# Strided sparse attention and a rational MLP on one core: smaller score blocks, fewer and larger transfers, PSUM banks handed out by the planner, |h| on ScalarE

## The chip, the cores and the metric

The kernel runs on one NeuronCore of a Trainium2 chip. The metric is device time in microseconds (us): the median of several executions of the same program. One further execution was recorded by the hardware profiler; its rows are quoted below. The engines are named as in the profile: PE (TensorE matmul), PEld (its weight loads), DVE (VectorE), ACT (ScalarE), POOL (GpSimd) and SP (SyncE, which computes nothing here and only issues transfers). A q behind an engine's name means its queue: SPq L455 is a transfer that SP issues at line 455.

## The reference

Batch 8, 8 heads, 576 positions, head size 64. The first four heads see the last 32 positions, the other four see the earlier positions with the same remainder by 32. The attention result, 4608 tokens of 512 numbers, goes through an MLP with a rational activation of 2048 hidden columns.

```python
scores = (1/np.sqrt(D)) * np.matmul(q, k.transpose(0, 1, 3, 2))
rel = pos[:, None] - pos[None, :]
mask_local   = (rel >= 0) & (rel < 32)
mask_strided = (rel >= 0) & (pos[None, :] % 32 == pos[:, None] % 32)
# heads 0..3 local, heads 4..7 strided; masked scores are -1e9
attn = softmax(scores)                      # max subtracted, sum + 1e-9
x = (attn @ v).transpose(0, 2, 1, 3).reshape(B * S, H * D)

h = x @ w_in                                # 4608x512 by 512x2048
P = a[0] + a[1]*h + a[2]*h*h + a[3]*h*h*h
Q = 1 + abs(b[0])*abs(h) + abs(b[1])*h*h
out = (P / (Q + 1e-6)) @ w_out              # by 2048x512
```

## The kernel before, in words

**Transfers.** POOL casts q, k and v of each batch to bf16 in DRAM scratch (lq, lk: local heads in pairs; sq, sk: strided heads; v), seven transfers a batch, and loads both weights. SP then loads each batch: lqT and lkT by four transposing transfers (L428), the values of the local heads vL by six (L433), sqT and skT by eight transposes, one for each head of q and of k (L440), and the values of the strided heads vS by 32 (L455), each of 18 rows by 4 heads. POOL copies sqT into an order that matmul can use (sqP, L445).

**Attention.** A batch has six units: four local heads and two pairs of strided heads. A local head is six blocks of 96 queries by 128 keys; a strided pair is six blocks of 54 by 54 for even and for odd positions. In each unit PE writes a mask through the identity matrix (L481, L534) and adds the scores (L487, L540), DVE takes row maxima (L493, L547), PE adds the negated maxima (L499, L554), ACT takes the exponential (L505, L560), SP transposes the probabilities from SBUF to SBUF (pL to ptL, L509; pS to ptS, L564), PE multiplies by the values with a column of ones beside them (ps_acc, L516, L574), and DVE divides by that sum (L522, L524, L581, L583). Results of local heads are transposed from SBUF into the MLP's input xt (L615, 57 transfers in all); strided ones go to DRAM by POOL (xs, L592) and come back by transposes (L623).

**MLP.** The tokens form nine chunks of 512. For each, PE makes 16 blocks of 128 hidden columns (ps_h, L641) and ACT evicts each to h (L645). Eight blocks are a group: DVE makes |h| by a bit mask (L656), then the denominator (L658, L660); ACT takes Ln and Exp of it (L661, L663), which is its reciprocal; DVE makes the numerator (L664 to L669) and the product (L670). The second matmul (ps_out, L683) collects 16 steps for each of four blocks of 128 tokens; ACT copies it out (L688) and POOL stores it (L694).

**What sets the order.** Every step is an operation with an engine, an estimated duration and a key. A planner in the kernel simulates the engines and picks on each the ready operation with the smallest key; the resulting order is written out, and each engine runs it strictly in that order, waiting on semaphores. SP's order is such a list as well, so a transfer whose data are late holds up all transfers behind it. PSUM is split into fixed rings: two score tiles of two banks (ps_s), one bank for ps_acc, two for ps_h, one for ps_out.

Of the kernel before, what the change touches and what calls it, by code (L numbers as in the profile page):

```python
# [22 lines left out]
class Op:  # L23

    __slots__ = ("eng", "maker", "dur", "deps", "key", "dst", "dma", "gen", "ndep", "users",
                 "ready", "fin", "cnt", "idx", "know")

    def __init__(self, eng, maker, dur, key, dst, dma):
        self.eng = eng
        self.maker = maker  # L30
        self.dur = dur
        self.key = key
        self.dst = dst
        self.dma = dma
        self.gen = None
        self.deps = {}
        self.users = []


class Tile:  # L40


    def __init__(self, name, t=None):
        self.name = name
        self.t = t
        self.prev = []
        self.w = []
        self.r = []
        self.gen = 0
        self.ndma = {}  # L50
        self.sem = None

    def new(self):
        self.prev = self.w + self.r
        self.w = []
        self.r = []
        self.gen += 1
        return self


class Prog:
# [6 lines left out]
    def op(self, eng, maker, dur, key, r=(), w=(), m=(), dma=None):  # L68
        o = Op(eng, maker, dur, key, None, dma)
# [7 lines left out]
        for t in m:  # L77
            for d in t.w + t.r:
                o.deps[d] = 1
        for t in r:  # L80
            t.r.append(o)
        for t in w:
            t.w.append(o)
        for t in m:
            t.w = [o]
            t.r = []
        if dma is not None:
            assert len(w) == 1
            o.dst = w[0]
            o.gen = w[0].gen  # L90
            o.dst.ndma[o.gen] = o.dst.ndma.get(o.gen, 0) + 1
# [3 lines left out]

    def schedule(self):
        for o in self.ops:
# [4 lines left out]
        pend = {e: [] for e in self.ENG}  # L102
        avail = {e: [] for e in self.ENG}
        free = {e: 0.0 for e in self.ENG}
        order = {e: [] for e in self.ENG}
        dmafree = 0.0
        for o in self.ops:
            if o.ndep == 0:
                heapq.heappush(pend[o.eng], (0.0, o.key, o.idx, o))
        left = len(self.ops)  # L110
        while left:
            best = None
            for e in self.ENG:
                if avail[e]:
                    t = free[e]
                elif pend[e]:
                    t = max(free[e], pend[e][0][0])
                else:
                    continue
                if best is None or t < best[0]:  # L120
                    best = (t, e)
            t, e = best
            while pend[e] and pend[e][0][0] <= t:
                _, k, i, o = heapq.heappop(pend[e])
                heapq.heappush(avail[e], (k, i, o))
            _, _, o = heapq.heappop(avail[e])
            free[e] = t + o.dur
            if o.dma is not None:
                dmafree = max(dmafree, t + o.dur) + o.dma
                o.fin = dmafree + 2.2  # L130
# [3 lines left out]
            left -= 1  # L134
            for u in o.users:
                lat = 0.07 if u.eng == o.eng else 0.15
                u.ready = max(u.ready, o.fin + lat)
                u.ndep -= 1
                if u.ndep == 0:
                    heapq.heappush(pend[u.eng], (u.ready, u.key, u.idx, u))  # L140
        self.order = order
        self.span = max(free.values())

    def emit(self):
# [26 lines left out]
        while len(done) < total:  # L171
            moved = False
            for e in self.ENG:
                while ptr[e] < len(self.order[e]):
# [5 lines left out]
                    for d in sorted(o.deps, key=lambda d: -d.idx):  # L180
                        if d.eng == "pe" and e == "pe":
# [10 lines left out]
                    ws = [(semof[s], n) for s, n in need.items()]  # L192
                    queues[e].append((ws, o))
# [3 lines left out]
            assert moved, "order is cyclic"  # L197

        def run(e):
            def go(eng):  # L200
                for ws, o in queues[e]:
# [5 lines left out]
                    elif inst is not None:  # L207
                        inst.then_inc(sems[e], 1)
            return go
        fin = {}  # L210
        for o in self.ops:
            if o.dma is not None and not o.users:
                fin[o.dst.sem] = max(fin.get(o.dst.sem, 0), o.cnt)

        def pool(eng):
            run("pool")(eng)
            for s, n in fin.items():
                eng.wait_ge(s, n)
        with nc.Block() as block:
            block.sync(run("sp"))  # L220
            block.gpsimd(pool)
# [5 lines left out]
class Ring:  # L227
    def __init__(self, tiles):
        self.tiles = tiles
        self.i = 0  # L230
# [6 lines left out]

def bass_strided_sparse_attn__then__act_rational_pade_kernel(nc, q, k, v, moe_w_in, moe_w_out, moe_a, moe_b, out):
    w_in, w_out, pa, pb = moe_w_in, moe_w_out, moe_a, moe_b
    B, H, S, D = q.shape  # L240
    Fin = H * D
    Fmid = w_in.shape[1]
    Fout = w_out.shape[1]
# [513 lines left out]
```

## Time and profile before

| | |
|---|---|
| median of 3 executions | 778.47 us (777.2 to 779.21) |
| profiled execution, span | 779.0 us |
| busy | PE 395.9, PEld 178.2, DVE 362.0, ACT 267.7, POOL 141.1 us |
| instructions | 6110, of them 2304 matmuls |
| DMA | 58.44 MB in 186076 packets, 179552 of them under 512 B |

The span is the time from the first to the last instruction of the profiled execution, and its own time; it lies 0.5 us above the median. A busy time is the sum over an engine's instructions; issuing transfers does not count as busy, so SP has no busy time, and what its queue costs shows in the chain of work that ended last (where SPq stands for SP's issuing) and in the waits for its transfers. In the slices, each digit is a fortieth of the span, in tenths busy. PE's clock is granted by a throttle; 1.00 is full speed.

### The profile page before, as it was taken

The numbers are of one execution on the slowest core, as the hardware profiler recorded it, in microseconds if no ns is written. First come the engines' busy times: TensorE is split into PE (matmuls) and PEld (weight loads), VectorE is DVE, ScalarE is ACT, GpSimd is POOL, SyncE is SP. The second block draws the span as 40 slices with busy tenths as digits, with TensorE's granted clock in tenths as the row PEclk, the third lists the DMA queues.
The fourth block names the chain that finished last, engine by engine and source line by source line (L and its number), as shares of the span: only waits on it lengthen the run. The fifth ranks groups of instructions, "written<-read, shape, count | busy, mean of one in ns | idle before, by whom it ended". The sixth has DMA issues, their size and how long they took to land.

```text
span 779.0 us, 6110 instructions
## 1 busy us (share of the span) xinstructions
PE 395.9 (51%) x2304; PEld 178.2 (23%) x2304; DVE 362.0 (46%) x353; ACT 267.7 (34%) x265; POOL 141.1 (18%) x184
## 2 busy tenths in 40 slices
PE   0212240401565010890169095789089959699864
PEld 0001120200222000340024042344034424233321
DVE  3000130100309104360298086489088959969960
ACT  0100000100126040262057044458138657577740
POOL 9007034005160100120003002022010400301100
PEclk9999999999997555795579588799579979999988
DMA  9999969218899042232301342352141321301011
GB/s 148 197 146 116 153 91 111 46 28 127 109 138 123 12 79 53 66 74 39 70 9 53 57 91 48 71 101 60 29 88 30 76 67 39 83 13 55 27 41 40
DMA packets 186076, 58.44 MB, mean 75 GB/s; under 512 B 179552, under 2 KB 182144, under 8 KB 185536
## 3 DMA queue, kind: packets, MB, share of 16 engines
q0 software_dynamic: 46144, 30.17, 23.3%
q1 hardware_dynamic: 139904, 27.90, 22.4%
q8 instruction: 18, 0.29, 0.2%
q14 instruction: 10, 0.08, 0.0%
HBM read 42.54 MB, written 25.95 MB: 88 GB/s over the span
## 4 chain that ended last, share of the span: by engine, by line
SPq 49%; PE 18%; DVE 17%; DMA 6%; ACT 4%; issue 4%; POOL 0%; DVEq 0%; ACTq 0%; POOLq 0%
SPq L455 24%; SPq L440 9%; PE ps_out L683 8%; PE ps_h L641 7%; SPq L615 7%; SPq L433 4%; SPq L428 4%; DVE z L666 3%; DVE z L668 3%; DMA ptL<-pL 3%; DVE h L670 2%; DVE u L660 2%; SPq L509 2%; DVE z L667 1%; ACT u L661 1%
## 5 line engine op out<-in xcount | busy, mean ns | idle before, releaser
L683 PE MATMUL ps_out<-Wout,h 128*128 128x512 bf16 x576 | 148.3, 411 | 25.6 <-ACT os L688 13.1
L641 PE MATMUL ps_h<-xt,Win 128*128 128x512 bf16 x576 | 144.2, 403 | 22.2 <-ACT h L645 9.4
L645 ACT ACTIVATE h<-ps_h 128x512 bf16<-128x512 f32 x144 | 85.0, 597 | 107.4 <-PE ps_h L641 107.3
L516 PE MATMUL ps_acc<-vL,ptL 128*96 128x65 bf16 x192 | 17.5, 237 | 165.3 <-DMA ptL<-pL 163.0
L505 ACT ACTIVATE pL<-ps_s 96x768 bf16<-96x768 f32 x32 | 25.7, 803 | 218.5 <-DMA ptL<-pL 121.4
L522 DVE RECIPROCAL rc<-ps_acc 96x6 f32<-96x6 f32 x32 | 6.1, 189 | 189.0 <-PE ps_acc L516 188.9
L694 POOL DMA_DIRECT2D out_dram<-os x36 | 26.5, 736 | 344.6 <-ACT os L688 340.2
L683 PEld LDWEIGHTS ps_out<-Wout,h 128*128 128x128 bf16 x576 | 57.0, 104 | 103.2 <-issue 17.1
L641 PEld LDWEIGHTS ps_h<-xt,Win 128*128 128x128 bf16 x576 | 52.0, 103 | 98.4 <-ACT h L645 30.4
L661 ACT ACTIVATE u<-u,consts 128x4096 bf16<-128x4096 bf16 x18 | 66.6, 3702 | 2.3 <-DVE u L660 2.2
L663 ACT ACTIVATE u<-u 128x4096 bf16<-128x4096 bf16 x18 | 65.1, 3618 | 0.1
L592 POOL DMA_DIRECT2D xs<-xS x48 | 35.4, 742 | 155.8 <-DVE xS L583 155.7
L493 DVE TENSOR_REDUCE ng<-ps_s 96x6 bf16<-96x768 f32 x32 | 30.3, 946 | 60.7 <-PE ps_s L487 60.6
L516 PEld LDWEIGHTS ps_acc<-vL,ptL 128*96 128x96 bf16 x192 | 15.6, 155 | 174.1 <-DMA ptL<-pL 166.9
L688 ACT ACTIVATE os<-ps_out 128x512 f32<-128x512 f32 x36 | 21.5, 596 | 98.6 <-PE ps_out L683 98.5
L481 PE MATMUL ps_s<-ML,IDN 128*96 128x512 bf16 x64 | 21.2, 423 | 57.4 <-DMA lkT<-lk 31.8
L445 POOL COPY sqP<-sqT 128x324 bf16<-128x324 bf16 x32 | 18.5, 620 | 128.0 <-DMA sqT<-sq 128.0
L390 POOL DMA_DIRECT2D lk<-in_k_dram x16 | 41.4, 3070 | 0.0
L524 DVE TENSOR_TENSOR xL<-ps_acc,rc 96x384 bf16<-96x384 f32 x32 | 17.6, 549 | 51.2 <-DMA xt<-xs 48.7
L660 DVE TENSOR_TENSOR u<-u,z 128x4096 bf16<-128x4096 bf16 x18 | 41.1, 2286 | 0.3
L666 DVE TENSOR_TENSOR z<-z,h 128x4096 bf16<-128x4096 bf16 x18 | 41.0, 2279 | 0.2
L670 DVE TENSOR_TENSOR h<-z,u 128x4096 bf16<-128x4096 bf16 x18 | 41.1, 2282 | 0.1
(41 smaller groups left out, 474.5 us busy)
## 6 DMA issues: line engine op xcount, KB each, us to landing
out_dram<-os POOLq DMA_DIRECT2D x36, 256.0 KB, 2.5
v<-in_v_dram POOLq DMA_DIRECT2D x8, 576.0 KB, 10.3
vS<-v SPq DMA_DIRECT2D x256, 9.0 KB
vL<-v SPq DMA_DIRECT2D x48, 64.0 KB, 2.2
lq<-in_q_dram POOLq DMA_DIRECT2D x16, 144.0 KB, 11.5
lk<-in_k_dram POOLq DMA_DIRECT2D x16, 144.0 KB, 11.3
sq<-in_q_dram POOLq DMA_DIRECT2D x8, 288.0 KB, 10.6
sk<-in_k_dram POOLq DMA_DIRECT2D x8, 288.0 KB, 11.8
```

The costliest lines, as they stand in the source:

```text
L390: P.op("pool", lambda e, s_t=s_t, d_t=d_t: e.dma_start(d_t[b, pair, :, :].rearrange("s (hh d) -> s hh d", hh=2), s_t[b, 2 * pair:2 * pair ...
L440: P.op("sp", lambda e, t=t, d_t=d_t, h=h: e.dma_start_transpose(t.t[:, h, 0:S // 2], d_t[b, h, :, :].rearrange("(c two) d -> c (two d)", t ...
L455: P.op("sp", lambda e, i=i, par=par, blk=blk, base=base: e.dma_start(vS.t[base:base + 52:3, blk // 2, par, :, blk % 2, 0:64], bass.AP(tens ...
L615: P.op("sp", lambda e, t=t, r0=r0, n=n, col=col, i=i: e.dma_start_transpose(t.t[:, 0:2, col:col + n], xl.t[r0:r0 + n, i, :]), 0.15, key + ...
L641: r = e.matmul(ph.t[:, :], Win[:, kk, f * 128:(f + 1) * 128], xt.t[:, kk, :], start=(kk == 0), stop=(kk == NK1 - 1))
L645: P.op("act", lambda e, f=f, ph=ph, h=h: e.activation(h.t[:, f % G, :], ph.t[:, :], AF.Copy), 0.53, key, r=[ph], w=[h])
L660: dv(lambda e, zz=zz, uu=uu: e.tensor_tensor(uu, uu, zz, op=Alu.mult), tt, r=[z], m=[u])
L661: P.op("act", lambda e, uu=uu: e.activation(uu, uu, AF.Ln, bias=eps1, scale=1.0), 0.833 * W / 1000 + 0.28, key, r=[T_co], m=[u])
L663: P.op("act", lambda e, uu=uu: e.activation(uu, uu, AF.Exp, scale=-1.0), 0.833 * W / 1000 + 0.19, key, m=[u])
L666: dv(lambda e, zz=zz, hh=hh: e.tensor_tensor(zz, zz, hh, op=Alu.mult), tt, r=[h], m=[z])
L670: dv(lambda e, zz=zz, hh=hh, uu=uu: e.tensor_tensor(hh, zz, uu, op=Alu.mult), tt, r=[z, u], m=[h])
L683: r = e.matmul(po.t[:, :], groups[g].t[:, j, m * 128:(m + 1) * 128], Wout[:, kk, :], start=(kk == 0), stop=(kk == NF - 1))
```

## The change

It alters the local and strided blocks, the transfers, PSUM, and the MLP's |h|:

- **Local heads** become 18 blocks of 32 queries by 64 keys, all four heads in one unit: 72 small matmuls (L522), placed in 32-column tiles of the array, with the mask for all of them by three matmuls through the identity (L509, L510), one maximum (L546), two exponentials (L559, L563) and one transpose of the probabilities (L566).
- **Strided heads** become blocks of 36 queries by 36 keys: positions with the same remainder by 16, one parity at a time (64 matmuls a batch, L591), in two units of two heads. PE reads every eighth column of sqT in place; the copies sqP are gone.
- **Weighted sums** are 72 matmuls for the local (L635) and 64 for the strided heads (L687), each half held back by a wait of PE for itself (`hard`).
- **Transfers**: a batch is loaded by four transposes (L469, L475), six vL (L481, L486) and eight vS (L495). All results go to DRAM (L665, L669, L696) and one or two transposes bring them back as xt (L711). SP also issues these stores and the output stores (L801); POOL keeps casts and weights. Casts of batch b+2 wait for the first load of batch b+1.
- **PSUM**: instead of fixed rings, the planner hands out one to three of eight banks to each result at the moment at which it orders the result's first operation, and makes that operation wait for the last users of those banks.
- **MLP**: ACT makes |h| for 16 of the 18 groups (L746); |h|, Ln (L759) and Exp (L764) run in halves of 2048 columns; the output matmuls (L789) are ordered in pieces of four instead of eight. Rings: xt 2 instead of 3, h 5 instead of 6.
- The planner's durations and keys are others: batch b's attention has the key 33b-20, chunk c's MLP 33c+10.

```diff
+class Banks:                        # n banks, place chosen when ordered
+    def __init__(self, n):
+        self.n = n
...
     def schedule(self):
...
+            if o.bank is not None:
+                b = o.bank
+                at, f = self._place(b.n, t)
+                b.at = at
+                for i in range(at, at + b.n):
+                    for d in self.blast[i]:
+                        o.deps.setdefault(d, 1)
+                    self.bfree[i] = 1e9
...
-        for h in range(HL):
-            for t, d_t in ((tq, sq), (tk, sk)):
-                P.op("sp", lambda e, t=t, d_t=d_t, h=h: e.dma_start_transpose(
-                    t.t[:, h, 0:S // 2], d_t[b, h, :, :].rearrange("(c two) d -> c (two d)", two=2)),
+        for nm, R, d_t, T in (("sq", R_sq, sq, T_sq), ("sk", R_sk, sk, T_sk)):
+            P.op("sp", lambda e, t=t, d_t=d_t: e.dma_start_transpose(
+                t.t[:, :, :], d_t[b, :, :, :].rearrange("h (c two) d -> (h c) (two d)", two=2)),
...
-        for i in range(16):
-            for par in range(2):
-                P.op("sp", lambda e, i=i, par=par, blk=blk, base=base: e.dma_start(
-                    vS.t[base:base + 52:3, blk // 2, par, :, blk % 2, 0:64],
+        for r in range(2):
+            for h in range(HL):
+                P.op("sp", lambda e, r=r, h=h: e.dma_start(
+                    vS.t[64 * r:64 * r + CS, h, :, 0:64],
...
+            return e.matmul(bank(SL, c + 64 - n, n, po, po + 32),
+                            lqt.t[64 * hh:64 * hh + 64, pair, LB * m:LB * m + LB],
+                            lkt.t[64 * hh:64 * hh + 64, pair, k0:k0 + n],
+                            start=False, stop=True, skip_group_check=True, tile_position=(64 * hh, po))
...
+                            r = e.matmul(bank(SS, 512 * j + CS * r2, CS, p, p + CS),
+                                         sqt.t[p:p + 64, h, r2:S // 2:8], skt.t[p:p + 64, h, r2:S // 2:8],
...
+        o1 = P.op("pe", lambda e: lav(e, 0), 36 * 0.028, key, r=[ptL, vl], w=[AL])
+        P.op("pe", lambda e: lav(e, 1), 36 * 0.028, key, r=[ptL, vl], m=[AL], hard=[o1])
...
             P.op("sp", lambda e, t=t, r0=r0, n=n, col=col: e.dma_start_transpose(
-                t.t[:, 2:4, col:col + n], xs[b, r0:r0 + n, :]), 0.15, key + 10, ...
+                t.t[:, :, col:col + n], xs[b * S + r0:b * S + r0 + n, :]), 1.25, key, ...
...
+    ABS_ACT = set(range(2, 18))
...
+            if c * NG + g in ABS_ACT:
+                for i in range(2):
+                    P.op("act", lambda e, z=z, h=h, i=i: e.activation(
+                        z.t[:, half * i:half * i + half, :], h.t[:, half * i:half * i + half, :], AF.Abs),
...
-            P.op("pool", lambda e, o=o, u0=u0: e.dma_start(out[u0:u0 + 128, :], o.t[:, :]), ...
+            P.op("sp", lambda e, o=o, u0=u0: e.dma_start(out[u0:u0 + 128, :], o.t[:, :]), ...
...
         if b + 1 < B:
-            st = loads(b + 1)
-        xl = attention(b, cur)
-        gather(b, xl)
+            st = loads(b + 1, b * PER + 8)
+        if b + 2 < B:
+            casts(b + 2, b * PER + 6, after=[P.ops[n0]])
+        attention(b, cur, b * PER - 20)
+        gather(b, b * PER - 2)
```

How the order moves, at three places. A row gives the line, the operation, what it writes and reads, the shape and the count. First SP, around the transposes that bring batch 0's results back as xt; before:

```order
L440 DMA_TRANSPOSE skT<-sk 128x288
L433 DMA vL<-v 128x4x64 x6
L509 DMA_TRANSPOSE ptL<-pL 128x6x96
L615 DMA_TRANSPOSE xt<-xL 128x2x96 x5
L615 DMA_TRANSPOSE xt<-xL 128x2x32 x3
L564 DMA_TRANSPOSE ptS<-pS 128x6x128
L428 DMA_TRANSPOSE lqT<-lq 128x576
L428 DMA_TRANSPOSE lkT<-lk 128x576
```

and after, where the loads of batch 2 stand ahead of them:

```order
L696 DMA xs<-xS 288x1x256 x2
L469 DMA_TRANSPOSE lqT<-lq 128x2x576
L469 DMA_TRANSPOSE lkT<-lk 128x2x576
L475 DMA_TRANSPOSE sqT<-sq 128x4x288
L475 DMA_TRANSPOSE skT<-sk 128x4x288
L481 DMA vL<-v 32x2x64
L486 DMA vL<-v 64x17x64 x2
L481 DMA vL<-v 32x2x64
L486 DMA vL<-v 64x17x64 x2
L711 DMA_TRANSPOSE xt<-xs 128x4x512
L711 DMA_TRANSPOSE xt<-xs 128x4x64
L495 DMA vS<-v 36x16x64 x8
```

Ten loads of batch 2 now precede the two transposes to xt, and eight follow them. Second, PE around the first weighted sums of batch 0; before, they come behind the scores of batch 0's strided pairs and among those of its later local heads:

```order
L534 MATMUL ps_s<-MS,IDN 128x384 x2
L540 MATMUL ps_s<-skT,sqP 54x54 x24
L554 MATMUL ps_s<-ng,IDN 118x384 x2
L516 MATMUL ps_acc<-vL,ptL 96x65 x6
L481 MATMUL ps_s<-ML,IDN 96x512
L481 MATMUL ps_s<-ML,IDN 96x256
L487 MATMUL ps_s<-lkT,lqT 96x128 x6
```

and after (L608 and L578 ahead belong to batch 0's strided heads and to batch 1's mask, L522, L591 and L553 to batch 1):

```order
L608 MATMUL ps<-ng,IDN 100x288 x4
L578 MATMUL ps<-MS,IDN 128x288 x4
L522 MATMUL ps<-lkT,lqT 32x64 x4
L522 MATMUL ps<-lkT,lqT 32x32 x2
L522 MATMUL ps<-lkT,lqT 32x64 x6
L522 MATMUL ps<-lkT,lqT 32x32 x2
L522 MATMUL ps<-lkT,lqT 32x64 x58
L591 MATMUL ps<-skT,sqT 36x36 x64
L553 MATMUL ps<-ng,IDN 128x512 x2
L553 MATMUL ps<-ng,IDN 128x128
L608 MATMUL ps<-ng,IDN 100x288 x4
L635 MATMUL ps<-vL,ptL 32x65 x36
```

Batch 1's whole scores now stand ahead of batch 0's first weighted sum (L635). Third, PE in the middle of the program, where MLP and attention alternate; before:

```order
L683 MATMUL ps_out<-Wout,h 128x512 x16
L499 MATMUL ps_s<-ng,IDN 96x512
L499 MATMUL ps_s<-ng,IDN 96x256
L516 MATMUL ps_acc<-vL,ptL 96x65 x6
L683 MATMUL ps_out<-Wout,h 128x512 x16
L481 MATMUL ps_s<-ML,IDN 96x512
L481 MATMUL ps_s<-ML,IDN 96x256
L487 MATMUL ps_s<-lkT,lqT 96x128 x6
L516 MATMUL ps_acc<-vL,ptL 96x65 x6
L683 MATMUL ps_out<-Wout,h 128x512 x16
```

and after:

```order
L789 MATMUL ps<-Wout,h 128x512 x4
L608 MATMUL ps<-ng,IDN 100x288 x2
L731 MATMUL ps<-xt,Win 128x512 x20
L608 MATMUL ps<-ng,IDN 100x288 x2
L731 MATMUL ps<-xt,Win 128x512 x16
L789 MATMUL ps<-Wout,h 128x512 x4
L635 MATMUL ps<-vL,ptL 32x65 x36
L731 MATMUL ps<-xt,Win 128x512 x4
L635 MATMUL ps<-vL,ptL 32x65 x36
L789 MATMUL ps<-Wout,h 128x512 x4
```

The first and second matmuls of the MLP (L731, L789) now alternate in pieces of four, and a batch's local heads pass as two runs of 36 instead of four of six.

More of the change, by code (lines that the diff above doesn't have):

```diff
@@ L79, in op @@
                 o.deps[d] = 1
+        for d in tuple(after) + tuple(hard):
+            o.deps[d] = 1
+        o.hard = hard
         for t in r:
@@ L101, in schedule @@
                 d.users.append(o)
[L102 to L105, printed above, removed]
+            for b in o.banks:
+                b.left += 1
+        self.bfree = [0.0] * NBANK
+        self.blast = [[] for _ in range(NBANK)]
+        ready = {e: [] for e in E}
+        free = {e: 0.0 for e in E}
+        order = {e: [] for e in E}
         dmafree = 0.0
@@ L139, in schedule @@
                 if u.ndep == 0:
[L140 removed]
+                    ready[u.eng].append(u)
         self.order = order
[L142 removed]
+        self.span = max(o.fin for o in self.ops)
     def emit(self):
@@ L197, in emit @@
             assert moved, "order is cyclic"
+        fin = {}
+        for o in self.ops:
+            if o.dma is not None and not o.users:
+                fin[o.dst.sem] = max(fin.get(o.dst.sem, 0), o.cnt)
         def run(e):
@@ L316, in bass_strided_sparse_attn__then__act_rational_pade_kernel @@
     R_o = ring("os", 3, [128, Fout], f32)
-    def ps(name, shape):
-        return nc.alloc_psum_tensor(name, shape, f32)
-    R_ps = Ring([Tile(f"ps{i}", ps(f"ps_s{i}", [128, 2, 512])) for i in range(2)])
-    R_pa = Ring([Tile("pa0", ps("ps_acc", [128, 512]))])
-    R_ph = Ring([Tile(f"ph{i}", ps(f"ps_h{i}", [128, 512])) for i in range(2)])
-    R_po = Ring([Tile("po0", ps("ps_out", [128, 512]))])
-    qi = np.arange(128)[:, None]
-    ki = np.arange(128)[None, :]
-    ml = np.full((128, NTL, 128), NEG, np.float32)
@@ new lines, in casts, with local, bulk @@
+    def casts(b, key, after=()):
+        for t in (T_lq[b], T_lk[b], T_sq[b], T_sk[b], T_v[b]):
+            t.new()
+        def local(pair, s_t, d_t, t):
+            P.op("pool", lambda e: e.dma_start(
+                d_t[b, pair, :, :].rearrange("s (hh d) -> s hh d", hh=2),
+                s_t[b, 2 * pair:2 * pair + 2, :, :].rearrange("hh s d -> s hh d")),
+                2.8, key, w=[t], dma=(1.2, 3.0), after=after)
+        def bulk(s_t, d_t, h0, nh, hd, t):
+            n = nh * S * D
@@ L697, in bass_strided_sparse_attn__then__act_rational_pade_kernel @@
-    casts(0)
-    weights()
-    for b in range(1, B):
-        casts(b)
+            if not hasattr(o, "st"):
+                o.st = Tile(f"st{o.name}")
+            o.st.new()
+            P.op("sp", lambda e, o=o, u0=u0: e.dma_start(out[u0:u0 + 128, :], o.t[:, :]), 0.5, ky + m * 7.6 + 7,
+                 r=[o], w=[o.st], dma=(0.8, 2.5))
+    PER = 33.0
+    casts(0, -100)
+    weights_in(0, -90)
+    weights_in(1, -89)
+    casts(1, -80)
+    gates = {}
     nxt = 0
-    st = loads(0)
-    pend = []
+    st = loads(0, -50)
```

815 lines of the change are left out of this document (431 added, 384 removed).

## The prediction

> **What bounds the kernel now.** I read the page's span, slices and chain first, then the SP queue line by line, the PE waits, two stretches, and last the durations that price the new parts.
>
> ```profile
> span 779.0 us, 6110 instructions
> ...
> PE   0212240401565010890169095789089959699864
> ...
> SPq 49%; PE 18%; DVE 17%; DMA 6%; ACT 4%; issue 4%; POOL 0%; DVEq 0%; ACTq 0%; POOLq 0%
> SPq L455 24%; SPq L440 9%; PE ps_out L683 8%; PE ps_h L641 7%; SPq L615 7%; SPq L433 4%; SPq L428 4%; DVE z L666 3%; DVE z L668 3%; DMA ptL<-pL 3%; DVE h L670 2%; DVE u L660 2%; SPq L509 2%; DVE z L667 1%; ACT u L661 1%
> ```
>
> The chain that ends last runs 49% through SP's queue: not through bytes, but through the time in which SP issues transfers. The costliest line is L455, the value loads of the strided heads. PE is nearly idle for the first 11 of 40 slices. What one issue costs (nanoseconds, min/median/max; the last row is the landing time of the ptL transposes in us):
>
> ```profile
> L428 SPq DMA_TRANSPOSE lqT<-lq x16: 1146/1263/11241, 11.2 to 527.9; - x16
> L433 SPq DMA_DIRECT2D vL<-v x48: 389/507/4978, 28.9 to 573.7; - x48
> L440 SPq DMA_TRANSPOSE sqT<-sq x32: 1149/1245/5744, 47.4 to 335.0; - x32
> L455 SPq DMA_DIRECT2D vS<-v x256: 737/741/1022, 41.6 to 560.5; - x128
> L509 SPq DMA_TRANSPOSE ptL<-pL x32: 1197/1237/4629, 80.1 to 669.7; - x32
> L615 SPq DMA_TRANSPOSE xt<-xL x57: 1159/1241/3992, 185.1 to 685.5; - x57
> L623 SPq DMA_TRANSPOSE xt<-xs x16: 1212/1264/1302, 218.9 to 673.1; - x16
> DMA to landing us min/median/max: 2.5/2.6/10.9
> ```
>
> A transpose costs SP about 1.25 us whether it moves 288x128 (L440), 576x128 (L428) or 512x256 (L623). With some 0.04 us between issues, a batch costs SP 4x1.30 (lq, lk) + 6x0.55 (vL) + 8x1.29 (sq, sk) + 32x0.78 (vS) + 6x1.29 (pt) + 57/8x1.28 + 2x1.30 = 63 us; eight make 504 us of the 779. Behind that queue PE waits for probabilities that are long computed:
>
> ```profile
> PE ps_acc L516 <- DMA ptL<-pL: 163.0, 10, 23.8
> ```
>
> Two stretches (length, busy us of PE, PEld, DVE, ACT, POOL, then the granted clock, DMA share, GB/s) show the middle, paced by SP, and the end, where SP is done and DVE works 104.27 of 112 us, 93%:
>
> ```profile
> 224.00:640.00 416.00, 237.00 (x1431) 108.65 (x1430) 222.77 (x216) 172.57 (x169) 53.98 (x73) 0.76 0.35 64
> 640.00:752.00 112.00, 92.61 (x442) 38.20 (x441) 104.27 (x75) 79.10 (x75) 14.99 (x18) 0.95 0.15 42
> ```
>
> **The change, part by part.** The prices of SP's start and of PE's work:
>
> ```profile
> 13.96 11.24 SPq L428 DMA_TRANSPOSE lqT<-lq  x1
> 25.24 3.58 SPq L428 DMA_TRANSPOSE lkT<-lk  x1
> 28.94 12.61 SPq L433 DMA_DIRECT2D vL<-v  x6
> ...
> 60.20 19.87 SPq L455 DMA_DIRECT2D vS<-v  x25
> 80.11 5.92 SPq L509 DMA_TRANSPOSE ptL<-pL  x2
> ```
>
> ```profile
> 224.43 15.48 PE L641 MATMUL ps_h<-xt,Win 128*128 128x512 bf16 x64
> ...
> 587.98 0.71 PE L540 MATMUL ps_s<-skT,sqP 64*54 64x54 bf16 x24
> ...
> 649.41 0.42 PE L516 MATMUL ps_acc<-vL,ptL 128*96 128x65 bf16 x6
> 649.67 3.62 PE L641 MATMUL ps_h<-xt,Win 128*128 128x512 bf16 x16
> 653.22 0.36 PE L574 MATMUL ps_acc<-vS,ptS 118*64 118x130 bf16 x6
> ```
>
> *SP per batch.* 4 load transposes, 3 of probabilities and about 2 gathers (15 in all): 9x1.30 = 11.7 us. 6 vL x0.55 = 3.3. 8 vS, each eight times the old one's bytes: between 0.55 (a 64 KB vL) and 2.1 (a vL of the congested start, 12.61/6); I take the median of the shape they are nearest to, 0.78: 6.3. The output stores and the xs stores, taken over from POOL, 4.5 + 5 at 0.55: 5.2. Sum 26.5 us against 63 (24 to 39 by the bounds). SP stops being the bound once an engine needs more than that per batch. POOL keeps only the casts; the sqP copies are gone. New is that SP stands still at an output store until ACT has made the copy, and behind it stand the next loads and the next gather, for which PE waits: 16 us of SP's slack a batch (PE's 43, below, less 26.5) cover that; without them each such wait goes straight to PE. The bytes grow (vS fills both partition halves, and all of x goes through DRAM instead of half of it); the DMA share of 0.15 to 0.35 in the two stretches hides that.
>
> *The first MLP matmul,* now at 224.43 us, waits for three batches of loads in SP's order. Loads of batch 0: lq and lk are the same bytes as the four old transposes, issued by 28.8 us. sq and sk: 12 (3 if uncongested, 17.6 at the rate of the first pair). vL: 8 (3 to 19). vS: 6. Three pt transposes: 4. That makes 59. Loads of batch 1: 4x1.30 + 3.3 + 6.3 = 15 clean, and about 7 more if casts are in flight, since the two ptL at 80.11 took 2.96 each instead of 1.24: 81. PE does batch 1's scores before batch 0's weighted sums, so SP next waits for landing, scores, maxima and exponentials: about 9, by which ptL(1) goes out at 90. xs stores and ptS: 6, so 96. Ten loads of batch 2: 8.5 clean, I take 12: 108. Gather: 2.6 and a landing of 2.5 to 10.9, say 6. First MLP matmul at **117 us** (100 if nothing is congested, 140 if everything runs at the worst rates).
>
> *PE from there.* A 512-column matmul at full clock takes (653.22-649.67)/16 = 0.222 us; 1152 of them 256 us. Per batch, attention has 272 small matmuls: 136 scores like L540, 0.71/24 = 0.030 each; 136 weighted sums between 0.030 and L574's 0.060, I take 0.035, because they stream 65 columns, not 130, and load 32 to 64 weight columns, not 96 as L516 does (0.26/6 = 0.043). Sum 8.8 (8.2 to 12.2). Masks and maxima: 4608 columns by identity at 0.222 per 512: 2.0. Four waits of PE for itself: 0 to 1, say 0.5. 11.3 a batch, with an eighth of the 256 43 us of PE. Batches 3 to 7 and the weighted sums of 1 and 2 remain: 5x11.3 + 2x5 = 66. Together **322 us**.
>
> DVE and ACT (busy us in all, mean ns of one, then idle time before):
>
> ```profile
> L660 DVE TENSOR_TENSOR u<-u,z 128x4096 bf16<-128x4096 bf16 x18 | 41.1, 2286 | 0.3
> ...
> L493 DVE TENSOR_REDUCE ng<-ps_s 96x6 bf16<-96x768 f32 x32 | 30.3, 946 | 60.7 <-PE ps_s L487 60.6
> ...
> L656 DVE TENSOR_SCALAR z<-h 128x4096 uint16<-128x4096 uint16 x18 | 21.9, 1216 | 18.5 <-ACT h L645 18.3
> L583 DVE TENSOR_TENSOR xS<-ps_acc,rc 118x384 bf16<-118x384 f32 x32 | 17.6, 551 | 0.3
> ```
>
> ```profile
> L645 ACT ACTIVATE h<-ps_h 128x512 bf16<-128x512 f32 x144 | 85.0, 597 | 107.4 <-PE ps_h L641 107.3
> L661 ACT ACTIVATE u<-u,consts 128x4096 bf16<-128x4096 bf16 x18 | 66.6, 3702 | 2.3 <-DVE u L660 2.2
> L663 ACT ACTIVATE u<-u 128x4096 bf16<-128x4096 bf16 x18 | 65.1, 3618 | 0.1
> L505 ACT ACTIVATE pL<-ps_s 96x768 bf16<-96x768 f32 x32 | 25.7, 803 | 218.5 <-DMA ptL<-pL 121.4 <-PE ps_s L499 96.9
> ```
>
> *DVE.* The nine MLP groups from L660 to L656 take 15.6 us for 8 x 512 hidden columns; without |h| 14.4. 18 groups: 259, plus two |h| left: 2.4. Attention by elements: 2304 of maxima at 946/768 and 3200 of normalising at 551/384, some 7.5 with the reciprocals; six batches: 45. **307 us**.
>
> *ACT.* 144 evictions and 36 output copies at 0.6: 108. Ln and Exp 18x7.32, in halves with some 0.15 more each: 137. |h| by ACT is not in the trace; the nearest row is Exp, 3618, so 16x3.8 = 61 (0 to 3 less). Exponentials 2.4x6 = 14. **320 us** at most, since neighbours overlap.
>
> The Trainium skill (ScalarE: Activation LUTs, Rules for kernel authors) says that simple elementwise work belongs on VectorE, which is up to about three times as fast in bf16. The rows agree: 1216 ns against about 3618. By that rule |h| stays on DVE, which then needs 327 us and would set the end some 5 us later than PE does; so here the move pays a little although each |h| gets three times as dear.
>
> *The sum.* After the start the three engines need 322, 307 and 320 us: PE is the longest, barely. At the 93% that the longest engine reached from 640 to 752: 322/0.93 = 346 (322 at 100%, 379 at 85%). Handing out PSUM banks when ordered costs no instruction; I give it nothing, since up to eight results can now be open where four rings of one or two tiles were, and if its planned times are off, PE waits for evictions, which the 93% is to cover. The end: after the last MLP-1 matmul comes a group's chain on ACT and DVE, under which PE still has earlier output matmuls; about 8 us stay open, and 4 for eviction, store and landing. 117 + 346 + 12 = **475 us**. The profiled span, 779.0, stands 0.07% above the median of 778.47, so nothing is scaled.
>
> **The rivals.** *Small matmuls at L574's 0.060 each:* 4.1 us more for a batch's scores and 3.4 for its sums; five batches and two of sums make 44: (322+44)/0.93 = 394, so 523 us. For it: 32-column tiles at changing array positions are in no row. Against: L540, whose tiles change rows too, at 0.030. The Trainium skill (TensorE: Matmul & The Clock Gate, the section on 56 against 53.3 ns) gives about 62 ns per matmul where its sequencer decodes in firmware and 25 as the floor otherwise; with 62 the time would be an estimated 526 us. L540's 30 ns speaks against that.
>
> *A late start:* casts of batches 2 and 3 are now tied to loads that stand before the gather, so they collide with them; if transposes go at the 11.24 us of the row at 13.96, the first MLP matmul comes at 165: 523 us. Against: later medians are 1.24 to 1.26.
>
> *The engines take turns:* with all three near full, each wait is another's; PE pauses, and the granted clock falls to the 0.76 of 224 to 640: 322/0.76 = 424, 553 us. For it: that stretch. Against: its pauses came from SP.
>
> *Better cover:* an early start, 100, and PE never waiting: 434 us.
>
> *Slower than before:* if a merged transpose held SP 11.24 us in every batch, as one did at 13.96, nine would cost 101 us, with the rest 116 a batch, 930 in all. It decides from about 7.3 us a transpose, (779-117-12)/8 = 81 us a batch. Against it: three sizes at one price.
>
> **How the numbers follow.** The forecast has 58% (445 to 505), small matmuls 8%, a late start 12%, turns 11%, better cover 8%, slower 2%, no change 1%. From 445 to 535 lie the forecast, most of the first two rivals, and about a third of the turns, the milder ones: 80%. About 0.3% is what a measurement of this kernel can tell from no change. Faster 0.97, same 0.01, slower 0.02.
>
> **What will show it.** Right: no SP line among the chain's first; the first L731 matmul at 100 to 140; PE, DVE and ACT each over 80% busy after it; L522, L591, L635 and L687 starting 0.027 to 0.045 apart; L469 and L475 issued in about 1.25. Wrong: L469 or L475 at several us, L687 at 0.06, the clock under 0.85 after the start, or PE waiting for a bank's release or for ptL.

## The result

The changed kernel takes 589.5 us (median of 6 runs, 581.5 to 597.7), the kernel before, beside it, 778.6 (777.2 to 779.2): a ratio of 0.750, 95% interval 0.746 to 0.754. The ratios, here and below, go by the runs that were not disturbed (here 581.5 to 588.4 us), and where a text below says how many us a run is faster or slower, that is a difference of ratios times 778.6 us. The forecast was 475 us with a range from 445 to 535. It missed by 114 us.

The page of the changed kernel (its span, busy time of the engines, PE and DMA in 40 slices, the two large queues, q1 with SP's transfers and q0 with POOL's, the chain that ended last):

```profile
span 586.6 us, 7831 instructions
...
PE 349.3 (60%) x3393; PEld 167.0 (28%) x3440; DVE 314.7 (54%) x227; ACT 306.6 (52%) x317; POOL 61.5 (10%) x64
...
PE   1012105103552379087796597994898899996846
...
DMA  9999999979999999979959995795214414000101
...
q1 hardware_dynamic: 171744, 43.84, 57.2%
q0 software_dynamic: 41408, 18.35, 27.8%
...
SPq 37%; PE 16%; DVE 16%; ACT 16%; DMA 12%; issue 4%; POOL 0%; ACTq 0%; POOLq 0%
SPq L495 10%; SPq L486 8%; PE ps L731 8%; PE ps L789 6%; DMA xt<-xs 5%; ACT z L746 5%; SPq L481 5%; DMA xs<-xS 4%; SPq L469 4%; SPq L475 4%; ACT h L735 4%; ACT u L759 3%; DVE u L755 3%; ACT u L764 2%; DVE z L770 2%
```

SP still leads the chain, and its first two lines are value loads: L495 (vS) and L486 (vL). The row of DMA slices stands near 9 for the first two thirds of the span and then drops; PE's digits stay at 8 or 9 only after that.

Stretches of the changed kernel (length, busy us of PE, PEld, DVE, ACT, POOL, granted clock, DMA share, GB/s): first everything from the first MLP matmul on, then two stretches with loads and one without.

```profile
152.60:586.60 434.00, 322.74 (x2773) 149.82 (x2816) 299.99 (x203) 298.24 (x304) 30.00 (x28) 0.87 0.72 97
200.00:240.00 40.00, 24.89 (x102) 10.30 (x104) 16.98 (x10) 20.84 (x24) 6.94 (x7) 0.80 1.26 131
280.00:320.00 40.00, 32.95 (x318) 16.85 (x322) 29.91 (x21) 30.03 (x31) 6.02 (x7) 0.91 1.08 139
480.00:520.00 40.00, 38.90 (x179) 17.42 (x181) 34.94 (x22) 37.30 (x38) 0.00 (x0) 1.00 0.19 55
```

The work that the engines have from the first MLP matmul on came out as priced: PE 322.7 us (forecast 322), DVE 300.0 (307), ACT 298.2 (320). What they do not have is each other's company: 434 us for it, not 358. With loads the DMA share is above 1, because the times of the two queues' packets add up in it (0.89 of q1 and 0.37 of q0 from 200 to 240 us). So 1 is no ceiling: the kernel below with all of vS contiguous reaches 1.50 in that stretch. PE is busy 25 to 33 of 40 us there, and 38.9 without loads.

What SP's issues cost there (ns, min/median/max):

```profile
L469 SPq DMA_TRANSPOSE lqT<-lq x8: 1269/1638/5493, 8.9 to 365.2; - x8
L475 SPq DMA_TRANSPOSE sqT<-sq x8: 1244/1572/9984, 20.0 to 369.0; - x8
L486 SPq DMA_DIRECT2D vL<-v x32: 573/684/10984, 33.4 to 385.4; - x32
L495 SPq DMA_DIRECT2D vS<-v x64: 757/1200/4128, 63.4 to 395.4; - x64
```

And a batch in SP's timeline (start, length, what): the value loads of batch 3 with a gather between, and the first load of batch 4.

```profile
179.99 0.53 SPq L481 DMA_DIRECT2D vL<-v  x1
180.57 7.38 SPq L486 DMA_DIRECT2D vL<-v  x2
187.99 1.17 SPq L481 DMA_DIRECT2D vL<-v  x1
189.20 1.86 SPq L486 DMA_DIRECT2D vL<-v  x2
191.10 9.57 SPq L495 DMA_DIRECT2D vS<-v  x6
200.72 6.30 SPq L711 DMA_TRANSPOSE xt<-xs  x2
207.07 1.58 SPq L495 DMA_DIRECT2D vS<-v  x2
208.70 1.54 SPq L469 DMA_TRANSPOSE lqT<-lq  x1
```

The value loads take 22 us of the 44 from batch 3's first load (at 164.5) to batch 4's; the gather that PE waits for stands behind six of the eight vS. Added up over the timeline, SP is occupied 365 of the 397 us up to the end of the last value load, 191 of them with value loads. The forecast had 26.5 us a batch for everything, 9.6 of it values; measured are 46 and 24. The transposes, priced 11.7 a batch, take 17.

PE's first MLP matmul, and three of the waits (us in total, times, longest):

```profile
152.61 9.25 PE L731 MATMUL ps<-xt,Win 128*128 128x512 bf16 x35 [10.21 <-DMA xt<-xs]
```

```profile
PE ps L522 <- DMA lkT<-lk: 79.4, 3, 28.0
DVE u L753 <- ACT z L746: 58.2, 13, 21.1
PE ps L731 <- DMA xt<-xs: 52.8, 7, 14.1
```

PE waits above all for the loads and for the gather. Waits whose releaser only frees a bank (L635 and L731 for the eviction L735, L789 for L658) add up to 22.5 us. DVE's wait for ScalarE's |h| is the largest sign of engines in turn.

### The profile page after: what moved, and what is told of

Read it like the earlier page. It is cut to its first block, busy times and chain, and to the rows that moved or that the text cites. A ratio compares the mean times of both kernels' runs of the same rounds, so it can differ in the third digit from the quotient of the medians.

```text
span 586.6 us, 7831 instructions
## 1 busy us (share of the span) xinstructions
PE 349.3 (60%) x3393; PEld 167.0 (28%) x3440; DVE 314.7 (54%) x227; ACT 306.6 (52%) x317; POOL 61.5 (10%) x64
## 3 DMA queue, kind: packets, MB, share of 16 engines
q1 hardware_dynamic: 171744, 43.84, 57.2%
## 4 chain that ended last, share of the span: by engine, by line
SPq 37%; PE 16%; DVE 16%; ACT 16%; DMA 12%; issue 4%; POOL 0%; ACTq 0%; POOLq 0%
SPq L495 10%; SPq L486 8%; PE ps L731 8%; PE ps L789 6%; DMA xt<-xs 5%; ACT z L746 5%; SPq L481 5%; DMA xs<-xS 4%; SPq L469 4%; SPq L475 4%; ACT h L735 4%; ACT u L759 3%; DVE u L755 3%; ACT u L764 2%; DVE z L770 2%
## 5 line engine op out<-in xcount | busy, mean ns | idle before, releaser
L731 PE MATMUL ps<-xt,Win 128*128 128x512 bf16 x554 | 149.1, 408 | 58.7 <-DMA xt<-xs 52.8
L789 PE MATMUL ps<-Wout,h 128*128 128x512 bf16 x553 | 149.9, 409 | 29.4 <-DVE h L776 17.0
L735 ACT ACTIVATE h<-ps 128x512 bf16<-128x512 f32 x144 | 82.0, 610 | 99.3 <-PE ps L731 98.4
L731 PEld LDWEIGHTS ps<-xt,Win 128*128 128x128 bf16 x576 | 56.3, 104 | 133.2 <-DMA xt<-xs 48.6
L789 PEld LDWEIGHTS ps<-Wout,h 128*128 128x128 bf16 x576 | 57.0, 104 | 101.5 <-DVE h L776 19.5
L759 ACT ACTIVATE u<-u,consts 128x2048 bf16<-128x2048 bf16 x36 | 70.6, 2000 | 19.3 <-DVE u L755 19.3
L764 ACT ACTIVATE u<-u 128x2048 bf16<-128x2048 bf16 x36 | 67.0, 1910 | 0.0
L428 POOL DMA_DIRECT2D lq<-in_q_dram x16 | 34.3, 2278 | 259.2 <-DMA lqT<-lq 258.4
L546 DVE TENSOR_REDUCE ng<-ps 128x18 bf16<-128x1152 f32 x8 | 10.8, 1356 | 93.5 <-PE ps L522 93.4
L746 ACT ACTIVATE z<-h 128x2048 bf16<-128x2048 bf16 x32 | 59.5, 1915 | 0.3
L522 PE MATMUL ps<-lkT,lqT 64*32 64x64 bf16 (+1 forms) x576 | 8.1, 207 | 79.6 <-DMA lkT<-lk 79.4
L559 ACT ACTIVATE pL<-ps 128x1024 bf16<-128x1024 f32 x8 | 8.2, 1019 | 79.9 <-PE ps L553 79.9
L773 DVE TENSOR_TENSOR z<-z,h 128x4096 bf16<-128x4096 bf16 x18 | 41.2, 2291 | 0.5
L770 DVE TENSOR_TENSOR z<-z,h 128x4096 bf16<-128x4096 bf16 x18 | 40.9, 2272 | 0.3
L591 PE MATMUL ps<-skT,sqT 64*36 64x36 bf16 x512 | 20.2, 245 | 25.1 <-DMA skT<-sk 25.1
L522 PEld LDWEIGHTS ps<-lkT,lqT 64*32 64x32 bf16 x576 | 6.0, 94 | 86.9 <-DMA lkT<-lk 81.0
```

Source lines behind the costliest of these rows:

```text
L428: P.op("pool", lambda e: e.dma_start(d_t[b, pair, :, :].rearrange("s (hh d) -> s hh d", hh=2), s_t[b, 2 * pair:2 * pair + 2, :, :].rearran ...
L731: r = e.matmul(bank(ph, 0, CH), Win[:, kk, f * 128:(f + 1) * 128], xt.t[:, kk, :], start=(kk == 0), stop=(kk == NK1 - 1))
L735: P.op("act", lambda e, f=f, ph=ph, h=h: e.activation(h.t[:, f % G, :], bank(ph, 0, CH), AF.Copy), 0.597, ky, r=[ph], w=[h], occ=0.494)
L746: P.op("act", lambda e, z=z, h=h, i=i: e.activation(z.t[:, half * i:half * i + half, :], h.t[:, half * i:half * i + half, :], AF.Abs), 1.9 ...
L759: lns.append(P.op("act", lambda e, u=u, i=i: e.activation(u.t[:, half * i:half * i + half, :], u.t[:, half * i:half * i + half, :], AF.Ln, ...
L764: exs.append(P.op("act", lambda e, u=u, i=i: e.activation(u.t[:, half * i:half * i + half, :], u.t[:, half * i:half * i + half, :], AF.Exp ...
```

## The experiments

Three theories. A: the 16 DMA engines are full until the loads end, above all with 128-byte packets. B: SP's queue is the price, its order or its issue time. C: PE, ACT and DVE take turns. Some kernels leave values out, so that their results are not the reference's; they only serve to price a part.

**Half of vS.** Each partition half gets only the columns that its sums read; the score columns are laid out accordingly.

```
-vS.t[64*r:64*r+CS, h, :, 0:64]               offset=(b*H+HL+h)*S*D          ap [D,16]
+vS.t[64*r:64*r+CS, h, 8*r:8*r+8, 0:64]       offset=((b*H+HL+h)*S + 8*r)*D  ap [D,8]
-score column CS*r2, weights block 4*j + r2//2, half r2 % 2
+score column CS*(2*(r2%4) + r2//4), weights block 4*j + r2%4, half r2 // 4
```

> Each of the two partition halves of vS gets only the 8 token columns that its weighted sums read, so the 8 vS loads of a batch have 288 packets of 128 B each and not 576; their count, their place in SP's queue and the arithmetic stay. Theory A (the 16 DMA engines are the bound until the loads end, through the many 128-byte packets): 18,432 packets fewer, at the 25 to 30 ns of engine time that one took in batch 1's loads, are 460 to 550 us of engine time, 29 to 35 us of sixteen engines: 550 to 562 us, with the loads ended near 360 us. Theory B (SP's order: xs stores and gathers stand behind the loads, and the issue of a load is what costs): the same number of issues, 575 to 592 us. Theory C (PE, ACT and DVE take turns, whatever the DMAs do): 585 to 592 us.

530.5 us (ratio 0.682, 0.677 to 0.687): 53 us less. C and B, as put down, expected next to nothing. A expected a gain, but 29 to 35 us: its direction came, and its size did not.

**Thin vS.** One column of 16; the other 15 are left out.

```
-vS.t[.., h, :, 0:64]    ap [16*D,CS],[D,16],[1,D]
+vS.t[.., h, 0:1, 0:64]  ap [16*D,CS],[D,1],[1,D]
```

> Each vS load brings one of its 16 token columns (the other 15 are left out and keep what they had), so the issues stay and nearly all of their packets go. Theory A: 34,560 packets fewer at 25 to 30 ns are 54 to 65 us of sixteen engines, 72 to 86 if only twelve carried them: 503 to 535 us. Theory B: if an issue itself costs SP the same with 36 packets as with 576, 570 to 592 us. Theory C: 585 to 592 us.

507.3 us (0.652, 0.648 to 0.655): 77 us less, in A's range. But an issue did not cost SP the same: the issues of vS, first in the halved kernel, then in the thin one.

```profile
L495 SPq DMA_DIRECT2D vS<-v x64: 367/474/4993, 64.0 to 344.0; - x64
```

```profile
L495 SPq DMA_DIRECT2D vS<-v x64: 315/366/2787, 61.4 to 323.7; - x64
```

At least 0.757 us with 576 packets, 0.367 with 288, 0.315 with 36: both edits cut SP's time along with the packets, so they cannot yet tell A from B.

**All |h| on VectorE.** `ABS_ACT = set()` for `set(range(2, 18))`.

> All |h| on VectorE again (1.22 us a group there, 3.8 us a group off ScalarE), all else as in the changed kernel. Theory A: hidden until the loads end, a few us either way, 582 to 594 us. Theory C (the wait of VectorE for ScalarE's |h|, 58 us in 13 waits, is what keeps the engines taking turns): the waits go, and some 25 to 50 us with them, 540 to 565 us. The prediction's own step said 5 us later when VectorE bounds.

584.9 us (0.751, 0.747 to 0.756), the same as the changed kernel. C, as far as ScalarE's |h| makes the engines take turns, falls as the cause of the miss.

**Stores on POOL.** The xs and output stores `P.op("pool", ...)` for `P.op("sp", ...)`.

> The xs stores (5 a batch) and the 36 output stores are issued by POOL, as before the change, and not by SP; the planner then orders anew. Theory A: the bytes and packets stay the same, 575 to 595 us. Theory B (a store waits in SP's queue behind the next batch's loads, 10 to 14 us in each of 8 batches): 500 to 550 us. Theory C: 585 to 592 us.

586.2 us (0.746, 0.739 to 0.753). The stores' place in SP's queue is not the price, though SP is rid of 76 issues.

**32 rows of 36,** on the halved kernel: `64 * r + 32` for `64 * r + CS`, `[16 * D, 32]` for `[16 * D, CS]`.

> On the kernel with halved vS loads (530.5 us): each vS load brings 32 of its 36 rows (the last 4 keys' V rows of every strided block are left out). 2,048 of its 18,432 vS packets go. The halving took 59 us away for 18,432 packets, 3.2 us a thousand. Theory A1 (all sixteen DMA engines share a 36-row transfer): 6.6 us less, 521 to 527 us. Theory A2 (36 rows are spread over 12 engines, 3 rows each, and 32 rows over 16, 2 each, so the busiest engines lose a third of their vS packets, as if 6,144 went): 20 us less, 505 to 514 us. This also is what would explain why halving gave 59 us where 29 to 35 were worked out for sixteen engines.

522.0 us (0.669, 0.665 to 0.674): 10 us less, nearer A1's 6.6 than A2's 20. By the Trainium skill (DMA: Bandwidth & Descriptors, the section on why a DMA increments its semaphore by 16) a transfer of 36 partitions runs on 12 engines and one of 32 on 16. The time shows no sign of it; which engine carried a packet no trace here shows.

**vS contiguous,** on the halved kernel: 2 loads a batch, spread by POOL.

```
-for h in range(HL): load vS.t[64*r:64*r+CS, h, 8*r:8*r+8, 0:64]
+load vW.t[64*r:64*r+CS, :, :]   ap [16*D,CS],[S*D,HL],[1,8*D]
+pool: tensor_copy(vS.t[0:NR, :, 0:8, 0:64], vW.t[0:NR])     once a batch
```

> On the kernel with halved vS loads: vS comes as 2 loads a batch of 36 rows by 4 heads by 1 KB, contiguous, into a buffer, and POOL copies it into the tile with the ones columns (one copy of 100 x 2048 a batch). 18,432 packets of 128 B become 2,304 of 1 KB, 64 issues become 16. Theory A (packets, not bytes, fill the DMA engines): as the run with thin vS or better, 498 to 512 us. Rival (bytes fill them): the bytes are the same, 525 to 532 us. Rival (POOL's copies hold VectorE up): above 520 us.

525.2 us (0.675, 0.669 to 0.680): the interval overlaps the halved kernel's, so no gain is shown, although SP's time on vS fell from 50 to 16 us. Either vS is no longer the price there, or POOL's copies cost what it saved; the run does not part the two.

**vL loaded once,** on the halved kernel.

```
-for hh: load block 0; for pair: load vl.t[64*hh:64*hh+64, pair, 1:NB]     64 rows
+for hh, pair: load vl.t[64*hh+32:64*hh+64, pair, 0:NB]                     32 rows
+for hh: pool: tensor_copy(vl.t[64*hh:64*hh+32, :, 1:NB], vl.t[64*hh+32:64*hh+64, :, 0:NB-1])
```

> On the kernel with halved vS loads: each V row of the local heads is loaded once (4 loads a batch of 32 rows by 18 blocks), and POOL copies the rows into the window half that holds the block before (2 copies of 32 x 2176 a batch). 35,840 packets of vL become 18,432, 48 issues become 32. Theory A: at 3.2 us a thousand 55 us less if these packets cost as those of vS did, at 25 ns over sixteen engines 27 us: 475 to 503 us. Theory C or a bound elsewhere by now: 520 to 530 us. Rival (POOL's copies, on the way of the casts in POOL's queue, delay them): above 530 us.

509.1 us (0.649, 0.645 to 0.653): 26 us less, close to the lower of A's two rates (27 us), though the median lies above A's range. A bound elsewhere, 520 to 530, falls.

**Wout later,** on the halved kernel: its two loads get `after=` batch 1's first load.

> On the kernel with halved vS loads: the two loads of Wout wait for batch 1's first load, as batch 2's casts do, and so leave the first 80 us. Same bytes in all. If the start alone is held up by them (the fourth vL load of batch 0 took 18 us, beside the weights): the first MLP matmul moves from 138 to 115 to 125 us and the end with it, 507 to 520 us. If it is the sum of all transfers that counts until the loads end at some 330 us: 524 to 534 us.

537.8 us (523.5 to 554.0; no interval). No gain, and a wider spread; in the profiled run the first MLP matmul came at 143 us, where the halved kernel has 138. Nothing shows that Wout holds up the start.

**All of vS, contiguous,** on the changed kernel: the same bytes as there, in pieces of 2 KB.

```
-64 loads of 36x16x64
+16 loads vW.t[64*r:64*r+CS, :, :]   ap [16*D,CS],[S*D,HL],[1,16*D];  two POOL copies a batch
```

> On the changed kernel itself: both partition halves still get all 16 token columns of vS, the same bytes as there (8 x 72 KB a batch), but as 2 loads of 36 rows by 4 heads by 2 KB, contiguous, and POOL spreads them in two copies a batch. 9,216... the 4,608 vS packets of 128 B a batch become 288 of 2 KB, 64 issues become 16. If packets fill the DMA engines: near the thin run, 505 to 530 us. If bytes fill them: 575 to 592 us. Between, 540 to 570 us, both count.

541.9 us (0.690, 0.684 to 0.696): 47 us less for the same bytes. The q1 queue (packets, MB, share) has the 43.84 MB of the changed kernel in 35,136 packets fewer:

```profile
q1 hardware_dynamic: 136608, 43.84, 58.3%
```

The Trainium skill (DMA: Bandwidth & Descriptors, Specifications) puts full rate at 512 B and more a piece. The run does not contradict it, but the time of q1's packets fell only from 336 to 310 us of 16 engines (shares times spans), and the edit also took 48 issues from SP, whose time on values fell from 191 to 89 us.

**Almost no V,** on the thin kernel: the large vL loads bring 1 block of 17.

```
-vl.t[64*hh:64*hh+64, pair, 1:NB, 0:64]   [LB*D, NB-1]
+vl.t[64*hh:64*hh+64, pair, 1:2, 0:64]    [LB*D, 1]
```

> As the run with thin vS, and the four large vL loads of a batch bring 1 of their 17 blocks (the other V rows are left out), so V takes next to nothing of the DMA engines; issues stay. If V's loads are all that stands between the forecast and the changed kernel: first MLP matmul at 110 to 120 us, and 470 to 487 us. If the casts (128-byte writes of lq and lk) and the transposes fill the engines too: 487 to 505 us, with a DMA share still near 1 until about 280 us.

493.9 us (0.636, 0.630 to 0.643). Its first MLP matmul, and all from there:

```profile
114.19 10.44 PE L731 MATMUL ps<-xt,Win 128*128 128x512 bf16 x36 [6.05 <-DMA xt<-xs]
```

```profile
114.20:489.50 375.30, 318.61 (x2818) 146.81 (x2818) 299.98 (x203) 296.83 (x304) 32.37 (x28) 0.93 0.50 96
```

The start lies at 114 us, where the forecast had 117. With the same work PE needs 375 us, not 434; the forecast had 358. PE's wait at L522 for lkT falls from 79.4 to 47.1 us and the one at L731 for the gather from 52.8 to 7.9. What is left of the transfers still counts: the time lies in the range put down for casts and transposes that load the engines too, and the DMA share is 0.80 and 0.89 in the two stretches from 200 to 280 us.

**Both V edits,** vS contiguous and vL once, the three POOL copies of a batch in a chain, in two runs:

> The two edits together (vS as 2 contiguous loads a batch and one POOL copy; vL loaded once and copied by POOL), the whole result computed. Theory A: V's packets fall from 72,704 to 20,736; 20 us below the run with contiguous vS (525) by what the copied vL took away from the halved one, 495 to 510 us. Rival (POOL's queue: three copies a batch that wait for loads stand ahead of the casts): 510 to 530 us.

> The kernel with both edits again (contiguous vS, vL loaded once, POOL copies), in more rounds, since four runs of it lay between 497 and 520 us: SP spent 59 us on V there for 200 in the changed kernel, and the run with nearly no V at all took 494. By both theories 495 to 510 us.

508.0 us (496.9 to 520.5, no interval), then 514.7 (0.659, 0.656 to 0.662). SP's time on values is 58 us, and it is no faster than vL loaded once alone. With all |h| on VectorE:

> As the run with both edits, and all |h| on VectorE. With the DMA engines no longer the bound the engines' own balance may show: VectorE gets 20 us, ScalarE loses 59. If VectorE and ScalarE bound it as the forecast had it: 2 to 8 us slower than the run with both edits. If VectorE's waits for ScalarE's |h| (48 us in 13 waits in the halved run) were time lost: 8 to 25 us faster.

503.1 us (0.643, 0.638 to 0.648), the lowest median of a kernel that computes the whole result. It lies within the spread of the first run above, but its interval is apart from the second's (0.656 to 0.662), so there |h| on VectorE may gain some 2%; where |h| should be is not settled. Against the changed kernel it is 83 us faster.

**SP's time back, few packets.** The thin kernel with each load in four issues, then in three, of one column each: `for c in range(4)` (or 3): `vS.t[.., h, c:c+1, 0:64]`.

> As the run with thin vS (1 of 16 columns for each of 64 loads), but each load is split into four, of one column each, so 4 of 16 columns come (the others are left out): 256 issues of 36 packets at the 0.32 to 0.37 us that an issue took in the thin run, 1.3 to 1.5 us in place of each vS load, what SP spent on it in the changed kernel (median 1.2 us), with a quarter of its packets (9,216 for 36,864). If SP's time for vS was the price: 565 to 592 us. If the DMA engines were: 507 to 525 us.

> As the run with four one-column issues for each vS load, with three (3 of 16 columns come): 192 issues, by interpolation between the thin run (36 us of SP's time on vS, 507 us) and the fourfold one (121 us, 597 us) some 90 us of SP's time, what the changed kernel spends on vS (89 us), with 6,912 packets for its 36,864. If SP's time on vS is the whole price: 580 to 595 us. If it is a part of it, by the same interpolation: 555 to 570 us, the rest being the engines'. If a threshold: below 540 us.

596.5 us (0.765, 0.760 to 0.770) and 564.0 us (0.722, 0.719 to 0.725). In the first, vS issues and two of the stretches:

```profile
L496 SPq DMA_DIRECT2D vS<-v x256: 290/366/4543, 65.3 to 417.9; - x128
```

```profile
200.00:240.00 40.00, 19.32 (x66) 7.35 (x67) 12.86 (x10) 9.02 (x11) 6.92 (x7) 0.65 0.77 98
280.00:320.00 40.00, 33.38 (x409) 17.02 (x409) 31.85 (x25) 28.40 (x30) 6.75 (x7) 0.91 0.91 114
```

The DMA share falls to 0.77 and 0.91 where the changed kernel has 1.26 and 1.08, and the time is no shorter than there; SP spends 121 us on vS, the changed kernel 87. A alone falls: SP's issue time is a price of its own. With three issues SP spends 93 us on vS (in its profiled run, which took 580 us), near the changed kernel's 87, and the time is 22 us shorter.

**vS issued by POOL,** whole (`P.op("pool", ...)` at L495), with two vS buffers, then with three:

> The changed kernel with its 64 vS loads, whole, issued by POOL and not by SP (POOL is busy 10% of the span there). Packets and bytes stay; SP loses 64 issues of 1.2 us. If SP's time for vS was the price: 520 to 550 us. If the DMA engines were: 572 to 600 us, and more if the loads, which POOL's queue issues in turn with the casts, hold the casts up.

> As the run with vS loaded by POOL, with three vS buffers in place of two: POOL's vS loads waited 86 us for the batch before last to be read, with the next casts behind them. If that wait was what ate the gain of taking vS from SP: 530 to 560 us. If the packets on the DMA engines were: 575 to 595 us.

585.9 us (0.752, 0.748 to 0.756) and 588.5 (0.756, 0.753 to 0.760): no gain from 64 issues less on SP. In the second, SP's issues of vL and two stretches:

```profile
L486 SPq DMA_DIRECT2D vL<-v x32: 573/755/19705, 33.0 to 392.6; - x32
```

```profile
200.00:240.00 40.00, 33.52 (x224) 15.21 (x229) 19.90 (x15) 24.06 (x29) 12.79 (x15) 0.87 1.31 127
240.00:280.00 40.00, 29.44 (x211) 13.48 (x213) 24.95 (x16) 24.27 (x28) 14.21 (x15) 0.87 1.45 146
```

The share rises to 1.45. Of the 87 us that SP no longer spends on vS, 47 come back at the same 48 vL issues (103 to 150 us) and 17 at the transposes (137 to 154), and the loads end at 393 us, where they ended at 397. This speaks against B alone as well, but less cleanly: the vS loads and the casts now wait in one POOL queue, and these runs do not take that out.

**What they have in common.** From the profiled runs: SP's time on values and in all, added up from its timeline up to the end of the last value load; and what is left of the span from there.

| kernel | SP on V, us | SP occupied of | rest of span | median, us |
|---|---|---|---|---|
| changed | 191 | 365 of 397 | 190 | 589.5 |
| vS by POOL, 3 buffers | 150 | 337 of 393 | 190 | 588.5 |
| thin vS, 4 issues | 230 | 394 of 418 | 183 | 596.5 |
| thin vS, 3 issues | 207 | 363 of 391 | 188 | 564.0 |
| all vS, contiguous | 89 | 298 of 340 | 192 | 541.9 |
| half vS | 139 | 306 of 344 | 181 | 530.5 |
| half vS, vL once | 103 | 280 of 330 | 183 | 509.1 |
| thin vS | 122 | 284 of 324 | 182 | 507.3 |
| almost no V | 72 | 250 of 304 | 186 | 493.9 |

(The row with three issues is of its run of 580 us, above the median.) The rest of the span is 181 to 192 us in each row, and 177 to 195 in the other nine profiled runs: the time follows the end of the loads. That end comes earlier where values take less of SP's time, but not in step: the second run with both V edits spends 58 us on values, and its loads end at 314 us, later than the 304 of almost no V.

## Why the prediction was wrong

The step that failed is "SP per batch", with its last sentence, "the DMA share of 0.15 to 0.35 in the two stretches hides that". That share came from a kernel that SP held back, and from two of its stretches; others of the same kernel stood far higher, 1.13 from 0 to 40 us and 0.96 from 200 to 240. Here the loads drive the share to 1.1 to 1.3 (the stretches above), and SP's issues get longer: the 64 vS, priced 0.78 each, take 1.2 in the median and 87 us in all (forecast 50), the 48 vL, priced 0.55, take 103 us (forecast 26). The same 48 vL issues take SP 86 us in the thin kernel and 150 where POOL issues vS, so their time goes by what else is in flight. SP remained the longest: occupied 46 us a batch until the loads end, not 26.5, beside the 43 that PE was priced at.

The prediction had the row that priced this. Its vL of the congested start took 12.61/6 = 2.1 each; the prediction used that for the upper bound of vS alone (its own terms make that bound 37, not 39), and kept vL at 0.55. Six vL at 2.1 are 12.6 us a batch; measured are 12.9.

*The sum, term by term.* Start: 117 forecast, 152.6 measured (+36); with almost no V 114.2. SP spends 26 us on values up to that point there, and the forecast's terms for values add up to about 27, so the other steps of the start add up as priced, with errors of some us each way. From there: 346 + 12 forecast, 434 measured (+76); with almost no V 375 (+17). The medians say the same: of the 114 us, 95 went with V (88 by the ratios) and 19 stayed. Nearly all of these are the 17, and so the 93%: less the forecast's 12 for the end, PE was busy 318.6 of 363 us there, 88%. Of its waits for a bank's release 18 us of the 22.5 remain, a term that the prediction put at nothing beyond the 93%. No experiment took that part further.

*How this divides* between SP's issue time and the packets is not fully settled. Thin vS took away 77 us; giving SP's time back without the packets (three issues) restores 55 of them, and the packets then make up the 22 to the changed kernel. But taking SP's time away and leaving the packets (POOL) gained nothing. The largest gains came from edits that relieve both. In the POOL runs the vS loads and the casts also wait in one queue, and that share was not taken out.

*The rivals.* The late start came in part (152.6 of its 165), but through value loads, and its price ended there, while in fact the rate after the start suffered too. Turns were forecast at a clock of 0.76 and 553 us; the clock was 0.87, but moving |h| in the changed kernel gained nothing and thinning V did, so the turns seem to have followed from the loads. Small matmuls at 0.060, rejected, did not come: 36 of L635 in 0.68 us (row below, from the kernel with almost no V) are 0.019 each. Over the whole changed kernel L635 is busy 8.7 us for 576 and L687 13.6 for 512, 0.015 and 0.027 each, both under the 0.035 taken. A merged transpose did not cost 11 us each time: medians 1.57 and 1.64, the longest 9.98.

```profile
107.46 0.68 PE L635 MATMUL ps<-vL,ptL 64*32 64x65 bf16 x36 [0.32 <-ACT pL L563]
```

*What held.* The work of PE, DVE and ACT within 7%. The sign: the kernel is 189 us faster by the medians. That the gain comes from SP's issues, 46 us a batch where the old kernel was priced at 63, fits, but no run takes the change's parts back one by one, so what each of them gave is not shown. *Of the signs:* SP lines lead the chain, L731 came after 140, and PE, DVE and ACT were busy 74, 69 and 69% after it: all three said that the forecast was wrong. The clock, 0.87, and the transposes' medians did not. The 5 us that |h| on ScalarE was to save did not show.

## What to carry to other kernels

When a change shortens the queue that issues transfers, price the transfers again in the DMA engines: count packets by size, and do not take the share of a kernel that was held back as room. Merging issues while loading data twice, in 128-byte pieces, trades one queue for the other. Load only what is read and load it once: halving vS gave 53 us, and loading vL once another 26. Fewer and contiguous pieces gave 47 us while vS was whole, and no gain that shows after it was halved. To tell two such queues apart, give each its load back alone; an edit that relieves both proves neither.

## What was not expected of the hardware

- An issue's time on SP grows with its packets even at its shortest: 0.315 us at least with 36, 0.367 with 288, 0.757 with 576. And the same instruction can take far longer: the vL issue took 0.573 to 19.7 us in the run with POOL and three buffers.
- POOL's copies seem to cost VectorE: the same 227 instructions were busy 315.2 us in the halved kernel and 328.6 in the one with 45 us of POOL copies of vL (the pages' rows, in this order). No run isolates it.

```profile
PE 346.5 (66%) x3440; PEld 163.9 (31%) x3440; DVE 315.2 (60%) x227; ACT 304.9 (58%) x317; POOL 63.6 (12%) x64
```

```profile
PE 344.8 (67%) x3440; PEld 164.9 (32%) x3440; DVE 328.6 (64%) x227; ACT 304.9 (59%) x317; POOL 109.1 (21%) x80
```
